# Seven early chunks, a split second unit, table copies on ScalarE and port waits in a WKV + cosine-MLP kernel

## The chip, the cores and the metric

The kernel runs on one core of a Trainium2 chip. Its time is the device time of one execution in microseconds (us). The engines of the core are TensorE (PE, matrix products), VectorE (DVE), ScalarE (ACT), GpSimd (POOL) and SyncE (SP, which here only issues DMAs). Each engine runs its own instructions strictly in order and waits at semaphores for the others.

## The reference

A linear attention with a decaying state (r, k, v: 4 batches, 8 heads, 768 tokens, 48 dims), and behind it an MLP over the 3072 tokens with a gate `h * cos(h)`:

```
for t in range(S):                       # S = 768, per batch and head
    cur = outer(u * k[t], v[t])
    y[t] = r[t] @ (state + cur)
    state = w * state + outer(k[t], v[t])
x = y as 3072 tokens x 384
h = x @ w_in                             # 384 -> 2048
g = h * cos(h)
out = g @ w_out                          # 2048 -> 384
```

## The kernel before

The recurrence is turned into products over chunks of 128 tokens: 24 chunks, 6 per batch, each of which gives one 128 x 384 piece of x. Four chunks make a block of 512 tokens, so there are six blocks. The MLP goes over steps: one step is one block and one slice f of 128 of the 2048 hidden columns, 96 steps in all. In a step PE makes `h` (9 products of 128x128 by 128x512, `mm_h`), DVE and ACT make g = h cos(h) in five passes and split it into a high and a low part (`gh` by ACT, `gl` by DVE, line 1413), and PE adds g @ w_out into accumulators (9 products, `mm_t`; in the last block `mm_o`). Every operand is split into a high and a low part in fp32r, hence three products for each.

The weights come in 32 pieces by DMA and are brought into shape and split by ACT, DVE and POOL while the first two blocks run (w_in piece f and w_out piece f must be there before step f of a block). To give this time, the first two blocks go alternately over parts of the hidden columns: `UNITS` lists (block, from f, to f). A unit that isn't the first of its block adds its result to the output with an accumulating DMA issued by POOL (line 1503); three DVE transposes (line 1488) bring its result into output form. 

A chunk with a number below `EARLY` = 8 is made in the early form: PE transposes r and k (`tr`, line 975), DVE multiplies them with decay tables (1029, 1040), PE makes scores (`mm_a`, 1094), DVE writes the causal ones over a diagonal that ACT has made from the u term (1076, 1099), PE makes the chunk's output X (`opens`, 1121 and 1132) and its state (`mm_z`, 1147). The u term of each chunk is two POOL products (1003, 1053) and a DVE sum (1059). Later chunks go in the late form: four loads each for r and k into staging buffers that the weights use too (932), DVE block transposes (987), POOL multiplies with late tables (993, 1215), PE makes scores and state sums together (`mm_az`, 1236 and 1244), DVE masks (1263) and PE makes X (1293). In both forms ACT then makes x's high part `xh` (1306) and DVE its low part `xl` (1311); the first h product of a block waits for all four chunks of its block. Block 0 is chunks 0 to 3 and block 1 chunks 4 to 7, so chunk 7 is the last that the first h of block 1 needs.

The order on each engine isn't left to a scheduler: every operation has a number in the table `PLACE`, a small planner turns the table into start times of its own and the operations are emitted in that order. In gaps that the planner sees on PE ahead of the first `mm_o`/`mm_t` it emits idle bf16 products of 128x128 (`warm_up`, line 1520) on a spare bank.

Ahead of everything PE opens six PSUM banks with bf16 products of 128x512 (`start_bank`, 527) and transposes w (539); DVE makes the powers of w (544) and from them the tables decT_k and decT_r (563); PE spreads u over the partitions (`u_all`, 645; ACT copies it as `u_b`, 651); PE and ACT make `dec_k` (595, 599). The late tables are copies of decT_k and decT_r moved to other partitions by 8 DMAs of SP (line 618).

## Time and profile before

| | us |
|---|---|
| device time, median of 3 runs | 494.9 (492.81 to 496.85) |
| device time of the profiled execution | 494.96 |
| its span in the trace | 493.2 |
| PE busy | 483.3 (98%) |
| DVE busy | 377.7 (77%) |
| ACT busy | 281.4 (57%) |
| POOL busy | 184.8 (37%) |

The span is counted from the first to the last instruction of the trace; 1.8 us of the execution's device time lie outside it. In the chain of work that ended last, PE has 91%. "Busy" of PE is the time in which a product is on its way; whether PE waits for others is told by the view of waits and by the starts of products one after the other.

### The profile page before, as it was taken

To read this page: it belongs to the slowest core of one execution; us is meant where nothing else is said; L and a number is where in the kernel's file an instruction comes from. 1 tells how busy PE (TensorE), PEld (TensorE's weight loads), DVE (VectorE), ACT (ScalarE), POOL (GpSimd) and SP (SyncE) were. 2 spreads that over 40 slices of the span, in tenths; PEclk is the share of its full clock that TensorE was granted. 3 is DMA by queue.
4 is the path that set the end of the run, shared out by engine and by line. 5 is a ranking of instruction groups with operands and counts; after the bars stand their busy time and mean duration, and the time that the engine had idled before them with its cause. 6 is when DMAs were issued, how large, how long until landed. Compare 5 with 4: busy or idle time off the path is not lost.

```text
span 493.2 us, 12086 instructions
## 1 busy us (share of the span) xinstructions
PE 483.3 (98%) x4698; PEld 395.5 (80%) x4698; DVE 377.7 (77%) x708; ACT 281.4 (57%) x644; POOL 184.8 (37%) x183
## 2 busy tenths in 40 slices
PE   8999999999999999999999999999999999999994
PEld 5877778888887878788888788888878878899894
DVE  7789999999989867876777888686977655664642
ACT  3688786667664734466456475565664635344441
POOL 6885435534556367346034261541133300000000
PEclk9999999999999999999999999999999999999999
DMA  6888548556875646766543553766554421110001
GB/s 120 181 179 167 161 139 199 150 150 173 186 169 110 118 69 114 131 127 156 136 111 67 135 118 100 144 185 161 109 133 97 113 72 32 33 33 1 1 1 69
DMA packets 145009, 57.36 MB, mean 116 GB/s; under 512 B 128046, under 2 KB 140848, under 8 KB 144944
## 3 DMA queue, kind: packets, MB, share of 16 engines
q1 hardware_dynamic: 140720, 54.94, 47.3%
q0 software_dynamic: 4224, 1.57, 3.3%
q8 instruction: 38, 0.62, 0.6%
q14 instruction: 27, 0.22, 0.2%
HBM read 49.81 MB, written 6.29 MB: 114 GB/s over the span
## 4 chain that ended last, share of the span: by engine, by line
PE 91%; DMA 3%; DVE 2%; SPq 1%; POOL 1%; issue 1%; ACT 0%; POOLq 0%; ACTq 0%; DVEq 0%
PE psum L358 39%; PE psum L374 33%; PE psum L365 7%; PE psum L1293 3%; PE psum L1236 2%; PE psum L1520 1%; PE psum L1244 1%; PE psum L1132 1%; DMA raw<-in_moe_w_out_dram 1%; SPq L905 1%; DMA raw<-in_moe_w_in_dram 1%; PE psum L975 1%; PE psum L1094 1%; PE psum L1121 1%; DMA early_r<-in_k_dram 0%
## 5 line engine op out<-in xcount | busy, mean ns | idle before, releaser
L358 PE MATMUL psum<-xh,w_in_hi 128*128 128x512 f32 x288 | 114.7, 398 | 0.1
L358 PE MATMUL psum<-xh,w_in_lo 128*128 128x512 f32 x288 | 113.0, 393 | 0.2 <-DVE w_in_lo L823 0.2
L358 PE MATMUL psum<-xl,w_in_hi 128*128 128x512 f32 x288 | 113.0, 392 | 0.0
L1410 ACT CAST gh<-psum 128x512 fp32r<-128x512 f32 x96 | 56.0, 583 | 70.5 <-PE psum L374 38.3
L374 PE MATMUL psum<-gh,w_out_hi 128*128 128x512 f32 x240 | 96.0, 400 | 0.0
L374 PE MATMUL psum<-gl,w_out_hi 128*128 128x512 f32 x240 | 94.0, 392 | 0.0
L374 PE MATMUL psum<-gh,w_out_lo 128*128 128x512 f32 x240 | 94.0, 392 | 0.0
L1413 DVE TENSOR_TENSOR gl<-psum,gh 128x512 fp32r<-128x512 f32 x96 | 65.7, 685 | 36.9 <-ACT gh L1410 36.3
L1215 POOL TENSOR_TENSOR T<-T,k 48x512 f32<-48x512 f32 x32 | 41.7, 1302 | 65.2 <-ACT T L1201 45.4
L358 PEld LDWEIGHTS psum<-xh,w_in_hi 128*128 128x128 f32 x288 | 54.1, 188 | 13.1 <-DVE gl L1413 0.9
L358 PEld LDWEIGHTS psum<-xh,w_in_lo 128*128 128x128 f32 x288 | 54.1, 188 | 12.7 <-DVE w_in_lo L823 0.9
L358 PEld LDWEIGHTS psum<-xl,w_in_hi 128*128 128x128 f32 x288 | 54.1, 188 | 10.9
L374 PEld LDWEIGHTS psum<-gh,w_out_hi 128*128 128x128 f32 x240 | 45.0, 188 | 10.7
L806 POOL TENSOR_TENSOR f<-f,raw 128x384 int32<-128x384 int32 x32 | 34.2, 1072 | 50.5 <-DVE f L795 26.2
L374 PEld LDWEIGHTS psum<-gl,w_out_hi 128*128 128x128 f32 x240 | 45.1, 188 | 10.0
L374 PEld LDWEIGHTS psum<-gh,w_out_lo 128*128 128x128 f32 x240 | 45.1, 188 | 9.1
L1201 ACT ACTIVATE T<-ident,a 128x128 f32<-128x128 f32 x128 | 41.6, 392 | 2.9 <-DVE a L1059 2.8
L1001 POOL TENSOR_TENSOR f<-f,f 128x384 f32<-128x384 f32 x16 | 16.7, 1042 | 67.3 <-DMA f<-in_r_dram 40.8
L377 ACT ACTIVATE decT_k<-psum 128x512 int32<-128x512 f32 x39 | 23.2, 595 | 26.1 <-PE psum L358 25.6
L1407 DVE TENSOR_TENSOR psum<-psum,decT_k 128x512 f32<-128x512 f32 x39 | 27.1, 694 | 11.1 <-ACT decT_k L383 10.8
L377 ACT ACTIVATE decT_r<-psum 128x512 int32<-128x512 f32 x38 | 22.7, 597 | 19.3 <-PE psum L358 19.1
L383 ACT ACTIVATE decT_r<-decT_r 128x512 f32<-128x512 f32 x38 | 23.9, 628 | 15.8 <-DVE decT_r L380 15.8
(159 smaller groups left out, 882.1 us busy)
## 6 DMA issues: line engine op xcount, KB each, us to landing
raw<-in_moe_w_out_dram SPq DMA_DIRECT2D x32, 384.0 KB, 3.4
raw<-in_moe_w_in_dram SPq DMA_DIRECT2D x32, 192.0 KB, 3.5
raw<-in_moe_w_in_dram SPq DMA_DIRECT2D x16, 384.0 KB, 4.0
raw<-in_k_dram SPq DMA_DIRECT2D x63, 80.0 KB, 2.8
raw<-in_r_dram SPq DMA_DIRECT2D x63, 80.0 KB, 2.5
out_dram<-o SPq DMA_DIRECT2D x21, 192.0 KB, 3.3
f<-in_k_dram SPq DMA_DIRECT2D x16, 192.0 KB, 3.6
f<-in_r_dram SPq DMA_DIRECT2D x16, 192.0 KB, 3.9
```

What stands on the lines that cost most here:

```text
L358: nc.tensor.matmul(ph, a, b_, start=(i == 0), stop=(i == len(mm) - 1))
L365: nc.tensor.matmul(acc, a[:, ts], b_, start=(first and i == 0), stop=(last and i == 2))
L374: nc.tensor.matmul(acc, a[:, ks], b_, start=(first and i == 0), stop=(last and i == 2))
L377: nc.scalar.activation(qi, ph, AF.Copy, scale=INV_2PI, bias=0.25)
L383: nc.scalar.activation(q, q, AF.Sin, scale=TWO_PI, bias=0.5 * math.pi)
L806: lambda: nc.gpsimd.tensor_tensor(ai(), ai(), cn(), op=ALU.add),
L1001: nc.gpsimd.tensor_tensor(mb(), rb(), kb(), op=ALU.mult)
L1201: nc.scalar.activation(to, ident2[:, None, :].to_broadcast([P, 2, SUB]), AF.Copy, scale=ab()[:, h : h + 1])
L1215: nc.gpsimd.tensor_tensor(M_(n)[rows], by_head(rT)[rows], b_late[1]()[rows], op=ALU.mult)
L1407: nc.vector.tensor_tensor(gb(), ph(), q(), op=ALU.mult)
L1410: nc.scalar.copy(gh(), gb())
L1413: nc.vector.tensor_tensor(gl(), gb(), f32(gh()), op=ALU.subtract)
```

## The change

- `EARLY` is 7: chunk 7 goes in the late form, chunks 0 to 6 in the early one.
- Block 0's second unit, f 4 to 16, becomes two: f 4 to 12 ahead of block 1's second unit, f 12 to 16 behind it. The accumulating output of block 0 happens twice: three more DVE transposes, four more accumulating stores on POOL.
- PE opens all six banks in a row, then transposes w, then makes 20 idle products (`o_warm`); `u_all`, `tab_t`, the first `tr`, `mm_a` and `mm_z` stand behind these. `WARM_AT` (until when the planner counts an idle product as slow) is 6.0 instead of 6.4.
- The late tables are made by eight ACT copies of 48x256 (`spread`) instead of eight DMAs; the small copy `swap_w` goes from DVE to ACT; the zeroing of the tables' buffers on POOL (630) moves behind the first chunk's product.
- In late chunks r's decay is one POOL product of 112x512 and two ACT copies of 48x512 (`place_r`) that put it in place, instead of two POOL products of 48x512; the mask is one DVE instruction of 128x1024 instead of two of 64x512.
- The last output tile is copied by ACT alone instead of by DVE and ACT, half each.
- Until the planner's time 180 a POOL instruction that reads or writes SBUF waits on a semaphore for the last preceding DVE instruction that needs the port which DVE and POOL share in the planner's model (`after_port`).
- The first state buffer of a batch is zeroed behind an earlier chunk's scores; `PLACE` is new throughout.

```diff
-UNITS = ((0, 0, 4), (1, 0, 8), (0, 4, 16), (1, 8, 16))
+UNITS = ((0, 0, 4), (1, 0, 8), (0, 4, 12), (1, 8, 16), (0, 12, 16))
-EARLY = 8
+EARLY = 7
-    3, 8, 11, 2, 4, 1, 6, 7, 14, 17, 18, 10, 13, 16, 24, 26, 28, 31, 262, 343, 89, 0, 201, 232, 12, 21, 25, 5, 9, 37,
...
+    3, 0, 7, 2, 4, 1, 6, 8, 10, 11, 13, 14, 16, 17, 18, 25, 28, 32, 36, 269, 206, 228, 26, 136, 30, 96, 38, 19, 27,
...
-WARM_AT = 6.4
+WARM_AT = 6.0
+PORT_UNTIL = 180.0
...
-        o_wT = op(PE, -95, 0.26, lambda: nc.tensor.transpose(b_w()[:, 0:NP], b_row()[0:NP, 0 : 2 * DP], ident[0:NP, 0:NP]), [o_w, o_wr, o_pool], [b_w, b_row], behind=o_banks[:2])
+        o_wT = op(PE, -95, 0.26, lambda: nc.tensor.transpose(b_w()[:, 0:NP], b_row()[0:NP, 0 : 2 * DP], ident[0:NP, 0:NP]), [o_w, o_wr, o_pool], [b_w, b_row], behind=o_banks)
+        o_warm = op(PE, -94, 2.2, lambda: warm_up(20), behind=[*o_banks, o_wT])
...
-        def late_table(b_, src):
-            def go():
-                for n in range(2):
-                    for j in range(2):
-                        at = (1 - n) * DP
-                        nc.sync.dma_start(
-                            b_()[at : at + D, j * NP : (j + 1) * NP, :],
-                            src[j * DP : j * DP + D, :, n * SUB : (n + 1) * SUB],
-                        )
...
+        def late_table(b_, src, n):
+            def spread():
+                for j in range(2):
+                    at = (1 - n) * DP
+                    nc.scalar.copy(
+                        b_()[at : at + D, j * NP : (j + 1) * NP, :],
+                        src[j * DP : j * DP + D, :, n * SUB : (n + 1) * SUB],
+                    )
...
-        o_up = op(PE, -23, 1.3, u_all, [o_ul, o_dve], [b_u, b_ub, b_ones], behind=o_banks)
+        o_up = op(PE, -23, 1.3, u_all, [o_ul, o_dve], [b_u, b_ub, b_ones], behind=[o_warm])
...
-                def decay_r(n):
-                    def go():
-                        rows = other(n)
-                        nc.gpsimd.tensor_tensor(M_(n)[rows], by_head(rT)[rows], b_late[1]()[rows], op=ALU.mult)
...
+                def decay_r():
+                    t = by_head(rT)[0:KP]
+                    nc.gpsimd.tensor_tensor(t, t, b_late[1]()[0:KP], op=ALU.mult)
...
+                def place_r(n):
+                    return lambda: nc.scalar.copy(M_(n)[other(n)], by_head(rT)[other(n)])
...
-                e_A = [op(DVE, due - 1.4, 0.74, mask(n), [o_A, o_pool2], [sp, M], some=True) for n in range(2)]
+                e_A = [op(DVE, due - 1.4, 1.27, mask, [o_A, o_pool2], [sp, M])]
...
-                        elif t == nt - 1:
-                            parts = (DVE, None, 0, 2), (ACT, SP, 2, 4)
...
+                if not o.port or o.start > PORT_UNTIL:
+                    continue
+                made = [i for i in nc.cur_bb.bb.instructions[before:] if i.engine == (nc.vector if o.eng == DVE else nc.gpsimd).engine]
+                if o.eng == DVE:
+                    held = made[-1]
+                elif held is not None:
+                    tc.add_manual_dep(made[0], held.name, after_port, reason="port")
+                    held = None
```

The table and the changed rules move rows on every engine. Three places show how.

DVE, from the last decay table on, in the kernel before (a_82 and a_83 are the u sums of chunks 0 and 1, `T<-psum,decT` the decayed r and k, `T<-upper,psum` the masks of the scores):

```order
L563 TENSOR_TENSOR decT_r<-pq,f_108 128x512
L1059 TENSOR_REDUCE a_82<-f_109 128x8
L1029 TENSOR_TENSOR T<-psum,decT_r 112x512
L1040 TENSOR_TENSOR T<-psum,decT_k 112x512 x2
L1029 TENSOR_TENSOR T<-psum,decT_r 112x512
L1099 COPY_PREDICATED T<-upper,psum 128x512
L1059 TENSOR_REDUCE a_83<-f_110 128x8
L1099 COPY_PREDICATED T<-upper,psum 128x512 x2
```

and in the changed kernel (lines are those of the changed kernel: 567 for 563, 1032 for 1029, 1043 for 1040, 1062 for 1059, 1102 for 1099):

```order
L567 TENSOR_TENSOR decT_r<-pq,f_107 128x512
L1032 TENSOR_TENSOR T<-psum,decT_r 112x512 x2
L1062 TENSOR_REDUCE a_82<-f_109 128x8
L1043 TENSOR_TENSOR T<-psum,decT_k 112x512 x2
L1062 TENSOR_REDUCE a_83<-f_110 128x8
L1102 COPY_PREDICATED T<-upper,psum 128x512 x3
```

The sum of chunk 0 stands behind both products with decT_r now, and the sum of chunk 1 stands ahead of the first mask instead of behind it.

ACT, its first instructions behind the table load, before (`T<-ident,a` are the diagonals of chunks 0 and 1):

```order
L651 COPY u_b<-psum 128x384
L599 COPY dec_k<-psum 128x4x2x48
L1076 ACTIVATE T<-ident,a_82 128x128 x8
L1076 ACTIVATE T<-ident,a_83 128x128 x8
L1076 ACTIVATE early_T_97<-ident,a_82 128x128 x4
```

and now (k_77 and k_78 are the buffers of the two late tables):

```order
L621 COPY k_77<-decT_k 48x256 x2
L654 COPY u_b<-psum 128x384
L603 COPY dec_k<-psum 128x4x2x48
L621 COPY k_78<-decT_r 48x256 x2
L1079 ACTIVATE T<-ident,a_82 128x128 x8
L1079 ACTIVATE T<-ident,a_83 128x128 x8
L1079 ACTIVATE T<-ident,a_82 128x128 x8
```

The first table copies stand ahead of `u_b` and the diagonals, and POOL's zeroing of k_77, on which they wait, has moved behind POOL's first product. On SP the load of u stands behind eight loads of r and k now, before behind four.

DVE, around the last things that the first h of block 1 waits for. Before, where chunks 6 and 7 are early:

```order
L1174 TENSOR_TENSOR s<-psum,pq 48x4x48 x2
L1029 TENSOR_TENSOR T<-psum,decT_r 112x512
L1099 COPY_PREDICATED T<-upper,psum 128x512
L784 TENSOR_SCALAR f_109<-raw_116 128x384
L1311 TENSOR_TENSOR xl<-psum,xh 128x384
L795 SCALAR_TENSOR_TENSOR f_109<-raw_116,f_109 128x384
L1099 COPY_PREDICATED early_T_97<-upper,psum 128x512
L1099 COPY_PREDICATED T<-upper,psum 128x512 x2
```

and now, where chunk 7 is late (L990 its second block transpose, of r; L1265 its mask; L1311 the low part of another chunk's x; its own stands four rows behind the last one shown):

```order
L990 STREAM_TRANSPOSE T<-raw_116 128x8x2x32
L1407 TENSOR_TENSOR psum<-psum,decT_k 128x512
L1311 TENSOR_TENSOR xl<-psum,xh 128x384
L1413 TENSOR_TENSOR gl_113<-psum,gh_111 128x512
L787 TENSOR_SCALAR f_110<-raw_117 128x384
L826 TENSOR_TENSOR w_out_lo_69<-f_107,w_out_hi_68 128x4x3x32
L798 SCALAR_TENSOR_TENSOR f_110<-raw_117,f_110 128x384
L382 SCALAR_TENSOR_TENSOR o<-psum,o 128x512
L1265 COPY_PREDICATED T<-upper_124,psum 128x1024
L1407 TENSOR_TENSOR psum<-psum,o 128x512
L1274 TENSOR_TENSOR w_101<-psum,v_80 48x8x48
```

Chunk 7's mask stands between the passes of the gate of two steps (382, 1407, 1413) and pieces of the weights (787, 798, 826). On PE its score products stand between `mm_t` products of steps that have been made by then, and its X with 15 such products around it ahead of the first h of block 1: 33 `mm_t` products stand ahead of that h now, 15 before.

## Rows read from the trace of the kernel before

**Rows 1.** PE's waits from the first h product to the last products.

```profile
engine line waited for: us in total, times, longest us
PE psum L1147 <- DMA early_v<-in_v_dram: 0.5, 1, 0.5
PE psum L358 <- DVE w_in_lo L823: 0.2, 1, 0.2
```

**Rows 2.** Chain of work that ended last: start, us, what.

```profile
65.86 2.06 PE psum L374 x9
96.67 1.03 PE psum L1293 x64
```

**Rows 3.** Timeline of PE, first steps: start, us, engine, line, operation.

```profile
32.50 0.50 PE L358 MATMUL psum<-xh,w_in_hi 128*128 128x512 f32 x1
...
35.34 1.11 PE L1094 MATMUL psum<-T 48*128 48x128 f32 x16
...
37.98 0.39 PE L975 MATMUL psum<-ident,early_r 64*112 64x64 f32 x8
...
38.52 1.08 PE L1121 MATMUL psum<-T,s 48*32 48x128 f32 x32
...
41.13 0.56 PE L1147 MATMUL psum<-early_v,early_r 128*48 128x48 f32 x16 [0.52 <-DMA early_v<-in_v_dram]
...
60.52 0.39 PE L358 MATMUL psum<-xh,w_in_hi 128*128 128x512 f32 x1
```

**Rows 4.** Line 1236 by windows: window, its length, PE busy, PEld busy.

```profile
84.00:100.00 16.00, 1.15 (x32) 1.01 (x32) 1.00 0.64 172
```

**Rows 5.** Timeline of DVE at the start.

```profile
15.25 0.75 DVE L1099 COPY_PREDICATED T<-upper,psum 128x512 f32<-128x512 int32 x1 [2.12 <-PE psum L1094]
15.88 0.55 DVE L1059 TENSOR_REDUCE a<-f 128x8 f32<-128x384 f32 x1
```

**Rows 6.** Timeline of ACT at the start.

```profile
7.26 0.48 ACT L651 COPY u_b<-psum 128x384 f32<-128x384 f32 x1 [4.92 <-PE psum L645]
...
9.99 2.45 ACT L1076 ACTIVATE T<-ident,a 128x128 f32<-128x128 f32 x8
...
16.46 2.45 ACT L1076 ACTIVATE T<-ident,a 128x128 f32<-128x128 f32 x8 [4.02 <-DVE a L1059]
```

**Rows 7.** The chain that ended last, at the start.

```profile
3.39 2.15 DMA f<-in_u_dram
```

**Rows 8.** Timeline of PE ahead of the first h.

```profile
7.15 1.56 PE L1520 MATMUL psum<-o 128*128 128x128 bf16 x13
...
15.96 0.90 PE L1520 MATMUL psum<-o 128*128 128x128 bf16 x13
...
20.48 1.08 PE L1121 MATMUL psum<-T,s 48*32 48x128 f32 x32
```

**Rows 9.** DMAs between 70 and 80 us: KB each, median us to landing.

```profile
raw<-in_moe_w_out_dram SPq DMA_DIRECT2D x1, 384.0 KB, 3.4
raw<-in_r_dram SPq DMA_DIRECT2D x4, 80.0 KB, 3.3
```

**Rows 10.** Page, groups of instructions: busy, mean ns, idle before.

```profile
L1215 POOL TENSOR_TENSOR T<-T,k 48x512 f32<-48x512 f32 x32 | 41.7, 1302 | 65.2 <-ACT T L1201 45.4
```

**Rows 11.** Timeline of DVE, a late chunk's mask.

```profile
88.89 1.51 DVE L1263 COPY_PREDICATED T<-upper,psum 64x512 f32<-64x512 int32 x2
```

**Rows 12.** Timeline of POOL, where staging buffers come free.

```profile
46.17 1.22 POOL L806 TENSOR_TENSOR f<-f,raw 128x384 int32<-128x384 int32 x1 [2.01 <-DVE f L795]
```

**Rows 13.** DVE and the others from 60 to 120 us, by windows: length, PE, PEld, DVE, ACT, POOL busy.

```profile
60.00:120.00 60.00, 59.91 (x379) 48.44 (x378) 58.65 (x113) 42.75 (x90) 28.55 (x27) 1.00 0.62 166
```

**Rows 14.** Timeline of DVE: two instructions of one kind, side by side.

```profile
79.90 0.52 DVE L823 TENSOR_TENSOR w_in_lo<-f,w_in_hi 128x384 fp32r<-128x384 f32 x1
80.34 1.66 DVE L823 TENSOR_TENSOR w_out_lo<-f,w_out_hi 128x384 fp32r<-128x384 f32 x1
```

**Rows 15.** Timeline of the end, all engines.

```profile
485.21 0.48 ACT L1432 COPY f<-psum 128x384 f32<-128x384 f32 x1 [2.59 <-PE psum L365]
...
485.74 0.89 DVE L1434 COPY f<-psum 128x384 f32<-128x384 f32 x2 [0.50 <-PE psum L365]
486.66 0.32 ACT L1432 COPY f<-psum 128x192 f32<-128x192 f32 x1 [0.97 <-DVE f L1434]
```

More of the change, by code (lines that the diff above doesn't have):

```diff
@@ L485, in start_pool2 @@
             )
+            nc.gpsimd.memset(upper2, 0)
             for i in range(2):
                 rows = slice(i * SUB, (i + 1) * SUB)
-                nc.gpsimd.tensor_copy(upper2[rows], upper[rows, rows])
+                nc.gpsimd.tensor_copy(upper2[rows, i], upper[rows, rows])
             for t in R_s:
@@ L606, in swap_w @@
                 rows = slice(j * DP, j * DP + D)
-                nc.vector.tensor_copy(wN[DP : DP + D, j * NP : (j + 1) * NP], pq[rows, :, NQ - 1])
-        o_wN = op(DVE, -20, 0.34, swap_w, [o_pow], port=True)
+                nc.scalar.copy(wN[DP : DP + D, j * NP : (j + 1) * NP], pq[rows, :, NQ - 1])
+        o_wN = op(ACT, -20, 0.5, swap_w, [o_pow])
         b_late = Buf(R_k[0:1]), Buf(R_k[1:2])
-        def late_table(b_, src):
-            def go():
-                for n in range(2):
-                    for j in range(2):
-                        at = (1 - n) * DP
-                        nc.sync.dma_start(
-                            b_()[at : at + D, j * NP : (j + 1) * NP, :],
-                            src[j * DP : j * DP + D, :, n * SUB : (n + 1) * SUB],
-                        )
-            return go
+        def late_table(b_, src, n):
[6 more added lines that the diff above has]
+                    )
+            return spread
         def start_w(b_):
@@ L634 @@
         o_late = [
-            op(SP, -5, 2.65, late_table(b_, src), [o_, o_lz], [b_, x], dma=0.4, first=-0.2, n_dma=4)
+            [op(ACT, -5, 0.8, late_table(b_, src, n), [o_, o_lz], [b_, x]) for n in range(2)]
             for b_, src, o_, x in ((b_late[0], decT_k, o_dtk, b_dk), (b_late[1], decT_r, o_dtr, b_dr))
@@ L995, in chunk @@
                 t_k = op(DVE, due - 2.9, 0.71, tr_s(kT, ks), [l_ks], [ks, kT])
-                e_k = op(POOL, due - 2.8, 1.3, decay_t, [t_k, o_late[0]], [kT, b_late[0]], port=True, some=True)
+                e_k = op(POOL, due - 2.8, 1.3, decay_t, [t_k, *o_late[0]], [kT, b_late[0]], port=True, some=True)
                 t_r = op(DVE, due - 2.8, 0.71, tr_s(rT, rs), [l_rs], [rs, rT])
@@ L1022, in chunk @@
                     [rb, kb, trp, rT, kT],
-                    behind=early_d[-2:-1],
+                    behind=[*early_d[-2:-1], o_warm],
                 )
@@ L1210, in stacked @@
                 ]
-                def decay_r(n):
-                    def go():
-                        rows = other(n)
-                        nc.gpsimd.tensor_tensor(M_(n)[rows], by_head(rT)[rows], b_late[1]()[rows], op=ALU.mult)
-                    return go
-                e_r = [
-                    op(POOL, due - 1.5, 1.3, decay_r(n), [t_r, *((o, 0.17) for o in o_d), o_late[1]], [rT, M, b_late[1]], port=True, some=True)
-                    for n in range(2)
-                ]
+                def decay_r():
+                    t = by_head(rT)[0:KP]
+                    nc.gpsimd.tensor_tensor(t, t, b_late[1]()[0:KP], op=ALU.mult)
+                o_r = op(POOL, due - 2.6, 1.3, decay_r, [t_r, *o_late[1]], [rT, b_late[1]], port=True, some=True)
+                def place_r(n):
+                    return lambda: nc.scalar.copy(M_(n)[other(n)], by_head(rT)[other(n)])
+                e_r = [op(ACT, due - 1.5, 0.59, place_r(n), [o_r, *o_d, o_pool2], [rT, M]) for n in range(2)]
                 def scores(n):
@@ L1522 @@
         order = plan.order(PLACE)
+        after_port = mybir.DependencyInfo(mybir.DependencyClass.Sync, mybir.DependencyReason.DATA)
+        held = None
         with tc.manual_schedule():
             for o in order:
-                if o.eng == PE and o_banks[0].end < o.start < first_o[0].start:
+                if o.eng == PE and o_warm.start < o.start < first_o[0].start:
                     cold = min(max(WARM_AT - (o.start - o.gap), 0.0), o.gap)
                     warm_up(max(int(cold / 0.112 + (o.gap - cold - 0.1) / 0.057), 0))
+                before = len(nc.cur_bb.bb.instructions)
                 o.emit()
+                if not o.port or o.start > PORT_UNTIL:
[5 more added lines that the diff above has]
+                    tc.add_manual_dep(made[0], held.name, after_port, reason="port")
+                    held = None
     ok = nc.values_load(flag, min_val=0, max_val=1)
```

25 lines of the change are left out of this document (12 added, 13 removed), and 189 rows, old and new, of the table PLACE.

## The prediction

> **What bounds the kernel now.** I read the waits of PE first, from its first h product on. Between 32.50 us [rows 3] and the last products there are only two, 0.5 us for a late load of v and 0.2 us for a piece of w_in [rows 1]. So from 32.50 us on PE is given work without a break for 453 us, and no other engine sets the end: whatever is to make the kernel faster must either bring the first h forward, or take work off PE behind it, or shorten the tail behind the last product. The chain of work that ended last gives the prices of that work: nine products `mm_t` take 2.06 us, 0.229 each, and a late chunk's X takes 1.03 [rows 2]. DVE is next: from 60 to 120 us it is busy 58.65 of 60 us [rows 13], and still PE lost nothing there. That is a warning that DVE has little to give in this stretch, not a bound.
>
> **Chunk 7 from early to late.** What PE does for an early chunk is read from the starts in its timeline [rows 3]: the transposes of r and k run from 37.98 to 38.52 (0.54), the scores took about 1.05 of the row of 1.11 before the next product started, X has two halves of which the first is the row at 38.52 (1.0 each by start to start, 2.0), and the state product at 41.13 takes 0.5. Together 4.1 us. The late form has no transposes on PE; its score products are busy for 1.15 us with the state products laid between them [rows 4], and X takes 1.03 [rows 2]. Two changes of shape between such products and the long ones cost PE about 0.2 each, an estimate: a 128x512 product takes 0.50 behind other work and 0.39 behind its own kind [rows 3], 0.11 for coming in and as much for going out. That makes 2.6. All of this stands behind the first h, in the stretch without a break, so **-1.5 us** if the products find their operands ready.
>
> **Whether they do.** The late chain is long, and the first h of block 1 waits for its end. In the order of the changed kernel that h, the fifth of all, has 33 `mm_t` products ahead of it where it had 15 before; it stood at 60.52 [rows 3]. Adding to the earlier first h (below) what the order puts between, 36 h products and 33 t products at 0.229 (15.8 us) and the early chunks' and chunk 7's work (some 14 us), I get about 60.8 for an h that never waits. Going back from there: chunk 7's staging buffers come free when POOL has converted a weight piece, and the product of that kind nearest to the place ended at 47.39 [rows 12]. From then: loads, 3.3 us to landing [rows 9] and up to 1.5 more for issuing the four; a block transpose on DVE (0.75 for a DVE pass over 128x512 [rows 5]); POOL's decay 1.30 [rows 10]; two copies by ACT (0.48 for 128x384 [rows 6], so about 0.6 each, an estimate); scores 1.15 [rows 4]; the mask 1.51 [rows 11] (one instruction over 1024 columns now, the same elements per lane as two over 512); X 1.03; xh and xl about 0.5 each. That is 12.9 us, which from 47.4 ends at 60.3, before any step of it has waited its turn on an engine. The order shows the mask behind gates and weight passes on a DVE that has 1.35 us to spare in 60. So it is just in time or a little late, and each us late is a us of PE. From below it costs 0, from above I take five steps that each wait for one instruction ahead of them, 5 us. I take **+1.0**, nearer to the lower end since 33 `mm_t` products lie ready to fill PE and the chain has about half a us of slack.
>
> **The start.** Chunk 0's and chunk 1's diagonals need sums with u. Before, u_b is there at 7.74, and 2.25 us later ACT begins the eight pieces of chunk 0's diagonal, at 9.99 [rows 6]. Chunk 1's sum stands on DVE behind the first mask, which waits 2.12 us for PE's scores [rows 5], so its diagonal begins at 16.46 and ends at 18.91 [rows 6], and chunk 1's X on PE follows at 20.48 [rows 8]. In the new order this sum is ahead of the mask, so ACT goes from the one diagonal straight to the other. Against it, u is loaded behind four more transfers: u's issue was at 3.39 behind five others [rows 7], so up to 0.68 each and 2.0 to 2.7 us later. The landing is then near 7.6, u_b near 10, chunk 0's diagonal at 12.2, chunk 1's ends at 12.2 + 4.9 = 17.1 instead of 18.91. This brings X of chunk 1 and what follows forward by 1.4 to 2.0. The end of the stretch, the first h, also needs three further chunks, which go by POOL and DVE at their old pace. I take **-1.5**, with 0 and -2.5 as ends.
>
> The six banks in a row and the 20 idle products keep PE busy where it waited for u before. Idle products took 0.12 each in the row at 7.15 (1.56 for 13) and 0.069 in the row at 15.96 (0.90 for 13) [rows 8]: the first is what the lower of the two clocks (1.2 GHz) gives and the second the upper (2.4 GHz), and the rise lies between. PE has no break in the new order up to the end of the 20 idle products, so the rise comes no later than before and perhaps earlier; real products before 14 us are few, so a gain from it is small, below half a us, and I count it as nothing. The Trainium skill, page "TensorE: Matmul & The Clock Gate", Part 1 (the clock gate), says that the array starts at the lower clock and goes to the upper after sustained work; the rows at the two rates agree.
>
> **Table copies.** Eight ACT copies of 48x256 cost ACT less than 0.48 each [rows 6], under 4 us in 30 in which it waits 4 and 5 us at a time for others [rows 6]. Eight transfers leave SP's queue. They aren't needed before chunk 7's decay. The price that could show is u_b behind the first pair, if POOL's zeroing is late: up to 1 us, in the range of the start.
>
> **Fifth unit.** Three more DVE transposes, 0.75 each by the nearest pass [rows 5], 2.2 us of DVE, and four stores on POOL, which has 28.55 of 60 us busy [rows 13]. PE does no more products. Weights f 12 to 15 are needed later than before, but PE never waited for such a piece beyond 0.2 us [rows 1], so the relief is worth nothing by itself. Cost 0, up to 2.2 if DVE were the bound there.
>
> **Port waits and late r.** Side by side, two DVE passes of one kind take 0.52 and 1.66 us [rows 14], the longer one while POOL works: 1.1 lost by DVE. The waits stop the reverse collision and leave DVE its time, so at most some of this comes back to DVE, which PE doesn't wait for: 0. What is queued behind a waiting POOL instruction is the next POOL product, and for it waits an early chunk's sum or a weight piece. The Trainium skill, page "SBUF — State Buffer", section on the two sides of SBUF, calls the shared port an exclusive lock, held for a whole instruction, the other side blocked; by that a semaphore only exchanges one block for another, and the sum would also get 0. One POOL product less in each late chunk (1.30 [rows 10]) and two ACT copies more are both beside PE's work.
>
> **Tail.** Before, DVE copies half of the last tile, then ACT the other half from 486.66 to 486.98, having waited 0.97 for DVE [rows 15]. ACT alone takes 0.48 [rows 15] from when the last products end, about 486.25: 486.75. **-0.2.**
>
> **Sum**, against the profiled execution's own 494.96 (the median, 494.9, is the same to 0.1): -1.5 (start) -1.5 (chunk 7) +1.0 (late chain) -0.2 (tail) = 492.8.
>
> **Rivals.**
> - *The late chain holds the fifth h* (slower). Place: the first h of block 1. From 3.2 us of lateness on, the gains are used up. With five steps each behind one more instruction, 5 us, 494.96 - 3.2 + 5 = 496.8. For it: 58.65 of 60 on DVE and a chain of 12.9 us in 13.4. Against: the 33 products ahead. Chance 0.20, of which 0.08 go beyond 1%.
> - *The start gains nothing, or the clock stays low*: 52 idle products stand ahead of the first scores; at the lower rate they take 52 x 0.051 = 2.7 us more than at the upper, and the scores come that much later, 495.5. Against: the rise came before 15.96 with less work ahead. Chance 0.07.
> - *Everything is hidden because DVE is the true bound* between 60 and 120 us: what PE gains it waits for DVE's gates later, in the same stretch; only the tail is left, 494.8. For it: 58.65 of 60; against: no wait of PE there. Chance 0.12.
> - *A larger gain*: the first h 2.5 earlier, no wait at the fifth: 494.96 - 2.5 - 1.5 - 0.2 = 490.8, and 489.5 with half a us from the clock and the 0.7 of waits [rows 1] gone too. Chance 0.20.
> - The forecast itself, 491.5 to 494: 0.41.
>
> **Range and chances.** The range goes from 489.5 to 497.0; it leaves out the worst of the late chain and little below. One per cent is 4.95 us, about what a measurement of this kernel can tell from no change. Faster than 490.0 needs nearly all of the larger gain: 0.16. Slower than 499.9 needs the chain to be over 8 us late: 0.08. Within: 0.76.
>
> **What would show it.** The first h at about 31.0; the fifth h at about 61 to 62 with a wait of about 1 us ahead of it or ahead of chunk 7's scores or X; PE's waits elsewhere below 1 us; from the fifth h to the last product the same length as before less the 18 `mm_t` products that moved ahead; the last copy ending 0.5 behind the last product. The prediction is wrong if chunk 7's rows (block transpose, decay, copies, mask) stand more than 3 us later than worked out, or if DVE shows up as releaser of PE's waits between 60 and 120 us.

## The result and the profile after

The changed kernel is slightly slower: 496.71 us median against 494.31, 20 runs of each, a ratio of 1.0054 with a 95% interval of [1.0039, 1.0069] (the quotient of the two medians alone is 1.0049). The forecast of 492.8 had the sign wrong; the time is within its range. The profiled execution took 496.11 (span 494.3), the one of before 494.96 (493.2).

| us | before | after | after - before |
|---|---|---|---|
| first h product | 32.50 | 32.65 | +0.15 |
| fifth h | 60.52 | 63.59 | +3.07 (18 `mm_t` more ahead: 4.1) |
| from the first h to the start of the last product | 453.39 | 454.10 | +0.71 |
| start of the last product | 485.89 | 486.75 | +0.86 |
| end of the last output copy | 486.98 | 487.60 | +0.62 |
| span | 493.2 | 494.3 | +1.1 |

The table covers this pair, which is 1.15 apart; the medians are 2.40 apart. The gain that was forecast for the first row isn't there, and the way from the first h to the last product is 0.71 longer where 0.5 less was forecast. The engines of after, busy by the page, and who had how much of the chain of work that ended last, after and then before:

```profile
PE 481.4 (97%) x4739; PEld 392.7 (79%) x4739; DVE 377.8 (76%) x693; ACT 304.0 (62%) x687; POOL 167.8 (34%) x174
...
PE 86%; DMA 4%; DVE 3%; SPq 2%; ACT 2%; issue 1%; POOL 1%; ACTq 0%; DVEq 0%; POOLq 0%
...
PE 91%; DMA 3%; DVE 2%; SPq 1%; POOL 1%; issue 1%; ACT 0%; POOLq 0%; ACTq 0%; DVEq 0%
```

PE has less of that chain, and loads, DVE, ACT and SP's issues have each a little more. Ahead of the first h the chain of before has one load in it, that of u; the chain of after has that of chunk 2's v too, for 5.23 us from its issue at 18.44 on. Where PE itself stands still, its waits tell; first up to 30 us, then from 30 us on (line, what it waited for, us in total, times, longest). Before, they were the two of [rows 1] from the first h on.

```profile
PE psum L1150 <- DMA v<-in_v_dram: 2.1, 1, 2.1
...
PE psum L648 <- DMA f<-in_u_dram: 0.5, 1, 0.5
PE psum L1124 <- DVE xl L1311: 0.3, 1, 0.3
...
PE psum L1238 <- ACT T L1222: 0.6, 1, 0.6
PE psum L376 <- DVE gl L1413: 0.4, 1, 0.4
PE psum L376 <- DVE w_out_lo L826: 0.2, 1, 0.2
PE psum L360 <- DVE w_in_lo L826: 0.2, 1, 0.2
```

The start in the timeline of after (start, duration, engine, what; in brackets the idle time ahead and its releaser; SPq are SP's issues):

```profile
17.89 1.08 PE L1124 MATMUL psum<-T,s 48*32 48x128 f32 x32
...
23.80 0.73 PE L1150 MATMUL psum<-v,early_r 128*48 128x48 f32 x16 [2.06 <-DMA v<-in_v_dram]
...
32.65 0.50 PE L360 MATMUL psum<-xh,w_in_hi 128*128 128x512 f32 x1
...
22.09 0.63 DVE L787 TENSOR_SCALAR f<-raw 128x384 int32<-128x384 int32 x2 [2.54 <-DMA raw<-in_moe_w_in_dram]
...
22.08 0.56 ACT L779 ACTIVATE raw<-raw 128x384 int32<-128x384 uint32 x1 [2.25 <-DMA raw<-in_moe_w_in_dram]
...
23.27 1.01 POOL L1006 TENSOR_TENSOR f<-early_r,early_k 128x384 f32<-128x384 f32 x1 [3.32 <-DMA early_v<-in_v_dram]
...
14.51 2.69 SPq L674 DMA_DIRECT2D raw<-in_moe_w_in_dram  x4
...
18.44 1.21 SPq L901 DMA_DIRECT2D v<-in_v_dram  x1
```

X of chunk 1 is 2.59 us earlier than in [rows 8], at 17.89. Then, between 19.7 and 24 us, PE, DVE, ACT and POOL all wait for loads, and the lead is gone. PE stood ready for chunk 2's v from 21.74 on. That load was issued at 18.44, and in the kernel before no later:

```profile
18.35 0.50 SPq L898 DMA_DIRECT2D v<-in_v_dram  x1
```

So the engines were earlier and the load was not. The windows (PE, PEld, DVE, ACT, POOL busy, clock, DMA share, GB/s) from 10 to 20 and from 20 to 30 us, first of the kernel before, then of after:

```profile
10.00:20.00 10.00, 10.00 (x194) 9.13 (x190) 6.41 (x13) 5.90 (x21) 9.67 (x10) 1.00 0.84 180
20.00:30.00 10.00, 9.85 (x248) 7.82 (x244) 9.11 (x20) 7.98 (x23) 7.34 (x8) 1.00 0.93 175
```

```profile
10.00:20.00 10.00, 9.97 (x234) 8.83 (x230) 8.51 (x16) 8.54 (x28) 9.87 (x11) 1.00 0.98 184
20.00:30.00 10.00, 7.61 (x180) 6.61 (x184) 7.51 (x17) 7.86 (x23) 5.70 (x6) 1.00 0.98 167
```

The 16 DMA engines are full (0.98) and move no more than before: 3.55 MB in these 20 us before, 3.51 after. The new `PLACE` also puts all four transfers of the first two w_in pieces (14.51) ahead of v of chunks 2 and 3; before, the second piece was issued at about 29.7 us.

In the late stretch ACT waits for a weight piece, and PE then for ACT and DVE:

```profile
65.59 0.56 ACT L779 ACTIVATE raw<-raw 128x384 int32<-128x384 uint32 x1 [3.33 <-DMA raw<-in_moe_w_out_dram]
66.05 2.43 ACT L1204 ACTIVATE T<-ident,a 128x128 f32<-128x128 f32 x8
...
70.51 0.61 ACT L1222 COPY T<-T 48x512 f32<-48x512 f32 x1
...
71.27 0.33 PE L1238 MATMUL psum<-T 48*64 48x64 f32 x4 [0.64 <-ACT T L1222]
...
73.72 0.50 PE L376 MATMUL psum<-gl,w_out_hi 128*128 128x512 f32 x1 [0.44 <-DVE gl L1413]
```

The diagonal (66.05) and the copies `place_r` (70.51) of chunk 8 stand behind the weight conversion in ACT's row, so a late transfer of a weight holds up a chunk that doesn't need it.

### The profile page after: what moved, and what is told of

Read it like the earlier page. It is cut to its first block, busy times and chain, and to the rows that moved or that the text cites. A ratio compares the mean times of both kernels' runs of the same rounds, so it can differ in the third digit from the quotient of the medians.

```text
span 494.3 us, 12169 instructions
## 1 busy us (share of the span) xinstructions
PE 481.4 (97%) x4739; PEld 392.7 (79%) x4739; DVE 377.8 (76%) x693; ACT 304.0 (62%) x687; POOL 167.8 (34%) x174
## 4 chain that ended last, share of the span: by engine, by line
PE 86%; DMA 4%; DVE 3%; SPq 2%; ACT 2%; issue 1%; POOL 1%; ACTq 0%; DVEq 0%; POOLq 0%
PE psum L360 37%; PE psum L376 32%; PE psum L367 7%; PE psum L1293 3%; PE psum L1238 2%; PE psum L1246 1%; DMA v<-in_v_dram 1%; DMA w<-in_v_dram 1%; PE psum L1518 1%; SPq L908 1%; DMA raw<-in_moe_w_in_dram 1%; DMA raw<-in_moe_w_out_dram 1%; PE psum L1150 1%; SPq L928 1%; DMA f<-in_u_dram 0%
## 5 line engine op out<-in xcount | busy, mean ns | idle before, releaser
L809 POOL TENSOR_TENSOR f<-f,raw 128x384 int32<-128x384 int32 x32 | 32.7, 1029 | 63.8 <-DVE f L798 21.7
L1204 ACT ACTIVATE T<-ident,a 128x128 f32<-128x128 f32 x136 | 44.3, 392 | 5.3 <-DVE a L1062 5.3
L1217 POOL TENSOR_TENSOR T<-T,k 112x512 f32<-112x512 f32 x17 | 23.9, 1407 | 45.8 <-DVE T L990 43.0
L996 POOL TENSOR_TENSOR T<-T,k 112x512 f32<-112x512 f32 x17 | 22.6, 1331 | 48.8 <-DVE T L990 47.7
L1407 DVE TENSOR_TENSOR psum<-psum,decT_k 128x512 f32<-128x512 f32 x35 | 24.3, 693 | 11.3 <-ACT decT_k L385 10.8
L379 ACT ACTIVATE decT_k<-psum 128x512 int32<-128x512 f32 x35 | 20.9, 598 | 17.9 <-PE psum L360 17.9
L379 ACT ACTIVATE decT_r<-psum 128x512 int32<-128x512 f32 x34 | 20.2, 596 | 18.4 <-PE psum L360 16.4
L1004 POOL TENSOR_TENSOR f<-f,f 128x384 f32<-128x384 f32 x17 | 18.7, 1098 | 35.1 <-DMA f<-in_r_dram 19.9
```

Source lines behind the costliest of these rows:

```text
L379: nc.scalar.activation(qi, ph, AF.Copy, scale=INV_2PI, bias=0.25)
L809: lambda: nc.gpsimd.tensor_tensor(ai(), ai(), cn(), op=ALU.add),
L996: nc.gpsimd.tensor_tensor(t, t, b_late[0]()[0:KP], op=ALU.mult)
L1004: nc.gpsimd.tensor_tensor(mb(), rb(), kb(), op=ALU.mult)
L1204: nc.scalar.activation(to, ident2[:, None, :].to_broadcast([P, 2, SUB]), AF.Copy, scale=ab()[:, h : h + 1])
L1217: nc.gpsimd.tensor_tensor(t, t, b_late[1]()[0:KP], op=ALU.mult)
```

## The experiments

Each ratio is to the kernel before, beside which each ran; after is at 1.0054. A ratio is not quite the quotient of the two medians, so differences between two runs are given as a range where the two disagree.

**e1_loads**: v of chunks 2 and 3 ahead of the second w_in piece.

```diff
-        order = plan.order(PLACE)
+        order = plan.order([{654: 80, 76: 56, 98: 57, 656: 133.5}.get(i, at) for i, at in enumerate(PLACE)])
```

> The changed kernel with one edit: on SP the loads of v for chunks 2 and 3 stand ahead of the second piece of w_in (and behind the first), and DVE's first pass over that second piece moves back by as much. Theory A (the start is held by the order of the loads: PE waits 2.1 us for a load of v at 21.7 us, DVE 2.5 and ACT 2.3 us for a piece of w_in): the wait for v goes below 0.5 us, the first h comes at 30.7 to 31.3 instead of 32.65, and the time falls by 1.2 to 2 us against the changed kernel, to 494.7 to 495.5. Rival B (the DMA engines are full between 10 and 30 us whatever the order): the wait moves to the next load, the first h stays at 32.4 to 32.9 and the time within 0.5 us. Rival C (the loss is behind the first h): first h earlier, time the same, with more waiting of PE behind it.

495.21, ratio 1.0019 [1.0005, 1.0034], so 1.5 to 1.7 us better than after. PE's wait fell from 2.1 to 0.5, but the first h came at 32.81. In its timeline part of the wait went to other loads:

```profile
22.64 0.56 PE L1150 MATMUL psum<-early_v,early_k 128*48 128x48 f32 x16 [0.51 <-DMA early_v<-in_v_dram]
...
27.19 0.55 DVE L1062 TENSOR_REDUCE a<-f 128x8 f32<-128x384 f32 x1 [2.85 <-POOL f L1056]
...
24.21 1.00 POOL L1006 TENSOR_TENSOR f<-early_r,early_k 128x384 f32<-128x384 f32 x1 [4.26 <-DMA early_r<-in_r_dram]
...
28.44 1.08 PE L1124 MATMUL psum<-T,s 48*32 48x128 f32 x32 [0.63 <-DVE T L1102]
...
31.54 1.46 PE L1518 MATMUL psum<-o 128*128 128x128 bf16 x23
...
33.62 0.50 PE L360 MATMUL psum<-xl,w_in_hi 128*128 128x512 f32 x1 [0.33 <-DVE xl L1311]
```

The u sum of a chunk (27.19) now waits through POOL for r, which came later instead of v. Still X of chunk 3, the last that the first h needs, began at 28.44, 1.10 earlier than in after (29.54). Why the first h didn't follow is not shown to be the queue: the planner had put 23 idle products (31.54) ahead of it that after doesn't have, and the second product then waited for an xl that stood on DVE behind a weight pass of 1.41 us (0.71 in after). So the run doesn't decide between theory A and rival B. The gain in the median goes with the clock: e1's mean clocks were 0.995 to 0.999, those of after 0.987 to 0.998.

**e2_noport**: without the port waits.

```diff
-PORT_UNTIL = 180.0
+PORT_UNTIL = -1.0
```

> The changed kernel without the waits of POOL for DVE. Theory A: no difference beyond 0.7 us either way; the first h stays at 32.65 within 0.3. Rival D (the waits hold POOL's first product, which starts at 6.60 behind a DVE instruction, and the u sums behind it): the first diagonal on ACT, at 11.92 now, comes 0.5 to 0.9 us earlier, and the time falls by as much if nothing else is late.

497.38, ratio 1.0059 [1.0044, 1.0073]: the time of after. Its profile caught a fall of the clock. After the wait ahead of chunk 2's state product 17 idle products took 2.00 us, in after 1.12; the windows behind (clock in the third figure from the right) show the lower level, 1.2 GHz.

```profile
23.91 0.73 PE L1150 MATMUL psum<-v,early_r 128*48 128x48 f32 x16 [2.12 <-DVE T L1102]
24.58 2.00 PE L1518 MATMUL psum<-o 128*128 128x128 bf16 x17
...
28.71 1.08 PE L1124 MATMUL psum<-early_T,s 48*32 48x128 f32 x32
```

```profile
24.00:26.00 2.00, 2.00 (x30) 1.86 (x31) 1.75 (x4) 2.00 (x7) 2.00 (x3) 0.64 0.88 160
26.00:28.00 2.00, 2.00 (x28) 1.71 (x27) 0.61 (x3) 2.00 (x6) 1.98 (x3) 0.51 0.67 130
```

That gives a price of one fall: from the state product to chunk 2's X it is 4.80 us here (23.91 to 28.71) and 3.33 in after's profile, where the clock stayed up (23.80 to 27.13), so about 1.5 us at this place. In e4, whose profile shows a fall too, it is 4.66.

**e3_fill**: 36 idle products in after ahead of chunk 2's state product, where PE waits.

```diff
+                if plan.ops.index(o) == 92: warm_up(36)
                 o.emit()
```

> The changed kernel with 36 idle products of 128x128 (about 2.0 us at the upper clock) ahead of chunk 2's state product, where PE waits 2.1 us for v. Theory E (in some executions PE's clock falls after this idle time, which makes the median run slower than the profiled one: its mean granted clock lay between 0.987 and 0.998): the mean granted clock of all runs stays at 0.995 or above and the median falls by 1 to 1.5 us against the changed kernel. Theory A without E: time and clocks spread as before, within 0.5 us.

494.79, ratio 1.0012 [1.0001, 1.0023]: 1.9 to 2.1 us less than after, by work that computes nothing. The mean clock was 0.996 to 0.998 in all 12 runs.

```profile
21.26 2.30 PE L1518 MATMUL psum<-o 128*128 128x128 bf16 x38
23.48 0.56 PE L1150 MATMUL psum<-v,early_r 128*48 128x48 f32 x16
...
31.80 0.50 PE L360 MATMUL psum<-xh,w_in_hi 128*128 128x512 f32 x1
```

The loads come about when they came (the state product at 23.48 against 23.80); what is gone is the pause, and with it the low mean clocks. In after's own runs the time goes with the mean clock, from 495.23 at 0.998 to 500.20 at 0.987. The size fits: 0.011 of 494 us less clock is 10.9 us at the lower level, which is 5.4 us of lost work (an estimate), against 5.0.

The mean has to be read with care. In after's profiled execution all that it lacks of 1 lies behind the last product (0.51 from 490.0 to 494.3), where it costs nothing; and a late rise at the start isn't in it (e10 below has runs near 498.5 at 0.997 and 0.998). The kernel before shows no such slope (494.8 at 0.989), and which stretch was low in those runs is open.

Nor is all of the 1.9 the clock: neither profiled execution, after's and e3's, shows a fall ahead of the first h, and yet it is 0.85 earlier in e3's. Of this 0.20 was there ahead of the pause already, 0.17 is the state product behind it (0.67 to the next start in after, 0.50 here), 0.33 is PE's wait for xl (the 0.3 among the waits above), and 0.12 the load. The Trainium skill, page "TensorE: Matmul & The Clock Gate", section "HAM oscillation — how this bites in real kernels", tells of a kernel whose clock falls back whenever its products wait for the next load; the rows of e2 agree in kind, though their wait, 2.12 us, is shorter than that kernel's.

**e4_act_order**: ACT's conversion of the late w_out piece behind chunk 8's diagonal.

```diff
-        order = plan.order(PLACE)
+        order = plan.order([{704: 329.5}.get(i, at) for i, at in enumerate(PLACE)])
```

> The changed kernel with one ACT instruction moved: the conversion of a w_out piece for which ACT waits 3.3 us at 62.3 us goes behind chunk 8's four diagonal groups. Theory F (this wait makes chunk 8's placing copies late, and through them PE's waits of 0.64 us at 70.6 and 0.44 at 73.3): both waits go, and the time falls by 0.8 to 1.2 us against the changed kernel. Rival: PE waits for the next thing on DVE instead, within 0.4 us.

495.77, ratio 1.0043 [1.0024, 1.0062]. PE's wait for `place_r` (0.64) is gone, and the way from first h to last product is 0.48 shorter (453.62 against 454.10). The wait for gl stayed at 0.4. The single profile again shows the clock at 0.50 from 24 to 26 us, here behind a wait of 1.66. So this wait was real but small, and only one of the two went that were to go.

**e7_before_port**: the kernel before with the port waits alone.

```diff
+                if o.eng == DVE:
+                    held = made[-1]
+                elif held is not None:
+                    tc.add_manual_dep(made[0], held.name, after_port, reason="port")
+                    held = None
```

> The kernel before with one part of the change alone: POOL's port instructions wait for DVE's, until the same time of the planner. Theory A: within 0.7 us of the kernel before. Rival D (the waits cost POOL its start): slower by 0.7 to 1.5 us, first h later than 32.50 by as much.

494.57 beside 494.57, ratio 1.0004 [0.9985, 1.0022]. With e2, the waits are worth nothing in either kernel that these runs can tell, to within about 0.9 us.

**e8_w1_late** and **e9_w1_late_act**: the second w_in piece seven loads later in after; e9 has e4's edit too.

```diff
-        order = plan.order(PLACE)
+        order = plan.order([{654: 119, 655: 160, 656: 160.2, 657: 160.4, 704: 329.5}.get(i, at) for i, at in enumerate(PLACE)])
```

(704 in e9 alone.)

> The changed kernel with the second piece of w_in (384 KB) loaded seven loads later, behind the last loads of chunk 6's r and k, and its ACT and DVE passes moved back; nothing else is put elsewhere. Theory B (the DMA engines are full between 10 and 30 us, 0.98 of the time, and the first h waits for what they bring): 384 KB less at 167 to 184 GB/s are 2.1 to 2.3 us, so the waits for v at 21.7 and for the first piece of w_in go, the first h comes at 30.4 to 31.3, the clock doesn't fall, and the time is 1.9 to 3 us below the changed kernel, 493.7 to 494.8. Rival C (something else in POOL's or DVE's order holds the start): first h at 32 or later. Rival G: the second h, at 43.33, waits for the piece that is late now, and gives the gain back.

> The run before with the ACT instruction of run e4 moved as well. Theory: both gains add, 0.5 to 1 us less than that run, 492.8 to 494.2, so that this is 0 to 1.3 us faster than the kernel before. Rival: chunk 8's placing copies aren't late any more once the start is earlier or later, and the two runs agree within 0.3.

e8: 495.17, ratio 1.0029 [1.0012, 1.0046], first h at 31.64. e9: 494.84, ratio 1.0012 [1.0001, 1.0023], first h at 31.33, 1.2 to 1.3 us ahead of both kernels. So 0.9 to 1.2 of the 1.5 us forecast for the start are there once the piece is out of the way; against e3, which kept the loads and filled the pause (31.80), it is 0.2 to 0.5. But with the start earlier, chunk 7 is late; from e9:

```profile
55.62 1.25 ACT L1222 COPY T<-T 48x512 f32<-48x512 f32 x2 [0.26 <-POOL T L1217]
...
54.29 1.30 POOL L1217 TENSOR_TENSOR T<-T,k 112x512 f32<-112x512 f32 x1 [2.02 <-DVE T L990]
...
57.01 0.33 PE L1238 MATMUL psum<-T 48*64 48x64 f32 x4 [0.67 <-ACT T L1222]
```

PE's scores waited 0.67 us there for these copies (0.46 in e8) and came 0.84 later than a product behind its own kind; the way from the first h to the last product is 454.53.

**e10_cold_start**: e3 with 1 instead of the 20 idle products behind the banks.

```diff
-        o_warm = op(PE, -94, 2.2, lambda: warm_up(20), behind=[*o_banks, o_wT])
+        o_warm = op(PE, -94, 2.2, lambda: warm_up(1), behind=[*o_banks, o_wT])
```

> Run e3 (36 idle products ahead of chunk 2's state product) with 1 idle product behind the six banks instead of 20. Theory A (the earlier rise of the clock, at 5 us instead of 13, is worth nothing): within 0.5 us of e3's 494.8, although the clock rises later. Rival H (the early rise is worth something): the scores of chunk 0 start later than 13.1 and the time is 0.5 to 2 us above e3's.

496.48, ratio 1.0043 [1.0017, 1.0069], 1.5 to 1.7 over e3, with runs near 495 and near 498.5. In the profiled one the planner's 52 idle products took 4.37 us (3.08 in after) and the first h came at 35.50:

```profile
12.35 4.37 PE L1518 MATMUL psum<-o 128*128 128x128 bf16 x52
```

So the price that the rival "the clock stays low" named is a real one, and the 20 idle products behind the banks keep it away.

**e11_r_first** and **e12_r_first_dve**: e9 with chunk 7's r loaded and decayed ahead of k; e12 also moves three DVE weight passes behind a gate.

```diff
+                if i == 7:
+                    l_rs = op(SP, due - 5.5, 2.5, load_s(rs, r), ahead, [rs], line=ln, dma=1.35, first=-0.1, n_dma=4)
+                    l_ks = op(SP, due - 5.8, 2.5, load_s(ks, k), ahead, [ks], line=ln, dma=1.35, first=-0.1, n_dma=4)
...
+        order = plan.order([{..., 188: 268, 190: 248, 189: 274, 199: 255, 201: 266.3, 200: 266.6, 19: 283.5, 680: 277.5, 712: 345.3, 706: 345.5, 713: 345.7}.get(i, at) for i, at in enumerate(PLACE)])
```

(The last three in e12 alone.)

> The kernel of e9 with one more thing moved: of chunk 7's two staged loads r goes ahead of k, and with it the transposes and the decay of r, and ACT's place copies of that chunk stand earlier in ACT's row. In e9 the first h came at 31.33 us, 1.3 us ahead of the kernel before and after, and chunk 7's state product az then waited 0.84 us for ACT's place copy, whose chain goes back to the load of r. Theory L (the late chunk's chain is the next limit once the start is earlier): the 0.84 us of az's wait falls under 0.3 us, the fifth h comes 0.5 to 0.9 us earlier than the 63.36 of e9, and the time is 0.4 to 0.9 us under that of e9: 494.0 to 494.4, a ratio of 0.9985 to 1.0005. Rival W (the wait is only moved): the same time is lost at a gate or at chunk 8's az, the fifth h comes within 0.3 us of 63.36, and the time is within 0.3 us of e9's.

> The kernel of e11 with three DVE passes over weights moved behind the gate after chunk 8's, so that the gate's own DVE work (gl) is not queued behind them at about 70 us, where PE waited 0.4 to 0.6 us for it in after, e4 and e9. Theory Q (the wait at the gate is a matter of DVE's row): the wait for gl falls under 0.2 us, and the time is 0.3 to 0.6 us under e11's, 493.4 to 494.0, with a ratio of 0.997 to 0.9995 to the kernel before. Rival: the three passes are then late for the products that read them (a wait for w_in_lo or w_out_lo of over 0.3 us between 70 and 85 us), or the gate waits for another operand, and the time is that of e11 within 0.3 us.

e11: 494.89, ratio 1.0007 [0.9984, 1.0030]; e12: 494.84, ratio 1.0003 [0.9981, 1.0026]. The wait at chunk 7 is gone and in e11 the fifth h is 0.62 earlier than in e9 (0.30 of it the first h was too), yet the way from the first h to the last product is 454.61 and 454.63. As the rival had it, the wait moved to the gates: 0.46 us for ACT's gh and 0.43 for DVE's gl in e11, 0.62 for gl in e12. In e12 gl stood behind the same three passes again, which I had put ahead of it.

**e13_before_less** and **e15_before_less_2**: the kernel before with its first w_out piece loaded behind chunk 4's v; e15 with the idle products as before.

```diff
-        order = plan.order(PLACE)
+        order = plan.order([{639: 105, 641: 130, 640: 134.5, 642: 136, 643: 144}.get(i, at) for i, at in enumerate(PLACE)])
...
-                    warm_up(max(int(cold / 0.112 + (o.gap - cold - 0.1) / 0.057), 0))
+                    warm_up({12: 3, 25: 4, 16: 13, 41: 30, 45: 13, 76: 11, 66: 5, 107: 5, 89: 1, 88: 1, 142: 1, 151: 5}.get(plan.ops.index(o), 0))
```

(The second hunk in e15 alone.)

> The kernel before with one thing moved: the first w_out piece (four transfers, 384 KB) is loaded behind the loads of chunk 4's v and not ahead of them. It asks what holds the first h of the kernel before at 32.50 us. Theory P (in the kernel before the start is held by work on the engines, so the loads became the limit only through the change): the first h stays at 32.5 within 0.3 us and the time is within 0.7 us of the kernel before. Rival B (the loads hold the start of both kernels, which is why the change's cheaper chunk 1 bought nothing): with 384 KB less ahead of it the first h comes 0.8 to 2 us earlier, and the time falls by 0.5 to 1.5 us unless a late w_out piece takes it back at the first output product.

> The kernel before with its first w_out piece (four transfers, 384 KB) loaded behind the loads of chunk 4's v, as in e13, and with the idle products of the kernel before at their old places, so none is added ahead of the first h. Theory P (in the kernel before PE's own row holds the start): the first h comes at 32.0 to 32.5 us, since PE's row ahead of it is the same work and ended at 32.20 in e13, and the time is within 0.7 us of the kernel before. Rival B (the loads hold the start of both kernels): the first h comes before 31.8 us.

e13: 497.43, ratio 1.0066 [1.0043, 1.0090]; 43 idle products (2.58 us) had come in ahead of the first h at 34.59, so it tells little of the loads. e15: 495.59, ratio 1.0033 [1.0012, 1.0054]. In its profiled execution the clock rose earlier (13 idle products in 0.90 at 6.13, against 1.56 at 7.15 in [rows 8]), the first scores began at 10.88 instead of 13.97, and PE then met what it had not met before:

```profile
6.13 0.90 PE L1520 MATMUL psum<-o 128*128 128x128 bf16 x13
...
15.13 0.56 PE L1147 MATMUL psum<-v,early_k 128*48 128x48 f32 x16 [1.10 <-DMA v<-in_v_dram]
...
31.18 0.49 PE L358 MATMUL psum<-xh,w_in_hi 128*128 128x512 f32 x1
33.49 0.50 PE L358 MATMUL psum<-xl,w_in_hi 128*128 128x512 f32 x1 [1.82 <-DVE xl L1311]
...
29.54 0.36 DVE L784 TENSOR_SCALAR f<-raw 128x384 int32<-128x384 int32 x1 [1.69 <-DMA raw<-in_moe_w_out_dram]
```

PE reached the first h 1.3 us earlier and its second product 0.65 later than before: the last xl of its block stood on DVE behind weight passes that had waited 1.69 for the piece that I had moved. Neither theory is shown by it: whether loads alone hold the start of the kernel before stays open. It does show that a lead of 3.1 us at the first scores can be lost to loads on the way to the first h.

**e14_gate_first**: e11 with the three passes behind the gl of that gate.

```diff
+        order = plan.order([{..., 712: 355.3, 706: 355.5, 713: 355.7}.get(i, at) for i, at in enumerate(PLACE)])
```

> The kernel of e11 with three DVE passes over weights moved behind the low half of the gate at about 71 us (in e12 they stood ahead of it). Theory Q (PE's wait for that low half is DVE's row): the low half ends 1.4 to 2.0 us earlier relative to chunk 8's XL, PE's wait of 0.6 us there falls under 0.1 us, and the time is 0.4 to 0.7 us under e11's 494.9: 494.2 to 494.5, a ratio of 0.9995 to 1.001 to the kernel before. Rival (the wait moves on to what the three passes make, w_in_lo and w_out_lo between 72 and 85 us): the wait for the gate goes, another of 0.3 to 0.6 us comes, and the time is e11's within 0.3 us.

498.24, ratio 1.0063 [1.0037, 1.0088], 2.8 to 3.3 us worse than e11. The wait for that gl (0.43 in e11, 0.62 in e12) is gone and 0.15 for its gh is left, but the next gate lost 0.86 and 2.02:

```profile
76.83 0.50 PE L376 MATMUL psum<-gh,w_out_hi 128*128 128x512 f32 x1 [0.86 <-ACT gh L1414]
79.59 0.80 PE L376 MATMUL psum<-gl,w_out_hi 128*128 128x512 f32 x1 [2.02 <-DVE gl L1417]
80.18 0.63 PE L376 MATMUL psum<-gh,w_out_hi 128*128 128x512 f32 x1
...
78.57 0.36 DVE L787 TENSOR_SCALAR f<-raw 128x384 int32<-128x384 int32 x1 [1.74 <-DMA raw<-in_moe_w_in_dram]
78.85 0.68 DVE L1417 TENSOR_TENSOR gl<-psum,gh 128x512 fp32r<-128x512 f32 x1
```

```profile
76.00:78.00 2.00, 0.74 (x2) 0.30 (x2) 0.83 (x2) 1.49 (x3) 1.92 (x3) 1.00 1.00 267
...
80.00:82.00 2.00, 2.00 (x6) 1.52 (x6) 2.00 (x5) 1.32 (x3) 0.68 (x1) 0.50 0.91 267
```

A gl that was ready to go stood on DVE behind a pass that waited 1.74 for its load. PE paused 2 us, and the clock was at 0.50 behind the pause: products of 0.40 took 0.63.

None of these is shown to beat the kernel before; e7, e11 and e12 can't be told from it.

## Why the prediction was wrong, point by point

- **The start, -1.5: the step that failed.** "The first h also needs three further chunks, which go by POOL and DVE at their old pace." The part up to chunk 1's X was right and cautious (2.59 earlier against 1.4 to 2.0). I then carried it to the first h without looking at the queue of the loads that the further chunks need (two, chunks 2 and 3, not three), nor at the share of the DMA engines, which was 0.93 between 20 and 30 us already. Chunk 2's v was issued at 18.44 as before at 18.35, so PE waited 2.06 for it, and the first h came 0.15 later: the term is off by 1.65. With the second w_in piece moved back (e8, e9) it came 1.0 and 1.3 earlier than after: most of the step holds when the loads let it.
- **The clock: not in the sum.** I looked at the clock only until its rise. Behind the wait for chunk 2's state product it fell again in the profiled executions of e2 and e4, for about 1.5 and 1.3 us each; after's own profile shows no fall (17 idle products in 1.12), and that some of its other runs fell there is read from their mean clocks and from e3, not seen. Filling the pause is worth 1.9 us in the median (e3); how much of this is the clock stays open, since 0.65 of it (0.85 less the 0.20 ahead of the pause) shows between two executions without a fall.
- **Chunk 7, -1.5: right.** Summed from start to start over all products from first h to last, the early kinds are 4.65 us shorter (scores 1.0, X 2.6, transposes 0.55, state products 0.5) and the late kinds 2.48 longer: -2.2. The 2.6 holds the wait of 0.52 for v [rows 3], which after doesn't have; without it the early work is 4.1, as forecast, and the late work 2.5 against 2.6.
- **The late chain and new waits, +1.0: mis-sized.** In the same sum `mm_h` takes 1.22 and `mm_t` 1.76 us longer, mostly as waits between 40 and 80 us: +3.0, which is 2.0 more than forecast. The chain of chunk 7 itself was in time (its scores at 57.24 waited for nothing; its steps add up to 12.7 us, not 12.9); the loss was at chunk 8's scores, at gates and at weight pieces. Of the +3.0 the four waits that PE's list shows behind the first h are 1.4 (0.2 before, the one for v aside), and e4 takes 0.5 back by one edit; what the rest would give back no run shows. I priced the chain of the chunk that is moved, not the rows of ACT and DVE that it is put into, where a late load stops everything behind it (e4, e14). -2.2 and +3.0 are the +0.7 of the table between first h and last product, forecast as -0.5.
- **Fifth unit 0, port waits 0, table copies 0: nothing speaks against them.** The port waits were tried (e2, e7), the other two not by themselves. PE waits for no weight piece behind 80 us. DVE didn't become the bound, but it is the releaser of two waits of PE between 60 and 120 us (0.4 for gl, 0.2 for w_out_lo), which the prediction had named as a sign of being wrong.
- **Tail, -0.2: right.** From the start of the last product to the end of the last copy 1.09 became 0.85. Behind the copy 0.50 more passed until the end; that stretch varied from 5.6 to 6.8 us over the executions profiled here.
- **The rivals.** "The late chain holds the fifth h" gave 496.8, the number nearest to the median, by luck: the fifth h waited for nothing, and the longest waits, 0.64 and 0.44, came behind it. "The start gains nothing" had the right outcome at the first h for a reason that was not the one: loads held it, and the clock wasn't low ahead of the scores. "DVE is the true bound" has 0.6 us of waits on its side, no more. Of "a larger gain" nothing came.

## What to carry to other kernels

Before the lead of one engine is carried on to a later point, follow every operand of that point back to its load, and read the DMA share of the stretch: at 0.93 it left no room for the lead here. In a row that an engine runs in strict order, look for the instructions that wait for a transfer, and count what is queued behind them as late as that transfer. A short pause of PE can cost more than itself; where a wait can't be removed, idle products that fit into it are cheap (e3). Those that a planner puts where PE doesn't wait are not: e13 has 42 more of them ahead of the first h than e15 and is 1.6 to 1.8 us slower. Count them in every run before reading its start.

## What the runs showed of the hardware

- PE idle for 1.66 to 2.12 us was followed by a stretch at the lower clock in e2, e4 and e14 (0.51, 0.50 and 0.50); after 2.06 in after's profiled execution and 1.82 in e15's it was not. What decides between them is open.
- The rise of the clock comes at different moments in executions of nearly the same row: in e15's at or before 6.13 us, in the kernel before's behind 7.15, and with one idle product instead of 20 (e10) behind 12.35. The clock of the windows reads 1.00 from the start in all of them, also from 6 to 9 us in the kernel before, where 13 idle products took 1.56: an early low stretch is read from the products' times, not from that figure.
- Full DMA engines moved 167 to 184 GB/s at the start, and 267 in e14 at 76 us. From 10 to 30 us after's loads are small packets:

```profile
DMA packets 14094, 3.51 MB, mean 176 GB/s; under 512 B 13260, under 2 KB 14028, under 8 KB 14089
...
v<-in_v_dram SPq DMA_DIRECT2D x3, 192.0 KB, 6.1
```

  That is 249 bytes a packet. The 6.1 us from issue to landing are of one load of v, that at 29.57; the one that PE waited for took 5.23, and in the kernel before loads of v took 5.1 in the same stretch, where the loads of [rows 9] took 3.3 and 3.4. The Trainium skill, page "DMA: Bandwidth & Descriptors", Specifications, gives 512 bytes as the least for full rate; no run here varied the packets.
